# Two score groups in a row in four PSUM banks, and the second head's P v summed at the pair's end

## The chip, the cores and the metric

The kernel runs on one core of a Trainium2 chip. A time is the device time of one execution in microseconds (us); the number for a kernel is the median of its runs. The core has five engines, each with an instruction stream of its own, in order: TensorE (PE, with its weight loads shown as PEld), ScalarE (ACT), VectorE (DVE), GpSimd (POOL) and SyncE (SP), which here only issues DMAs. Matrix products go to PSUM, eight banks of 128 partitions by 512 fp32 values; ACT and DVE read them there.

## The reference

```
q, k, v: (8 batches, 12 heads, 448 tokens, 64), fp32;  g_q, g_k: (64)
q_n = q / rms(q) * g_q ;  k_n = k / rms(k) * g_k
scores = q_n k_n^T / 8 ;  attn = softmax(scores) ;  o = attn v
x = o, as 3584 tokens by 768
h = x w_in  (768 by 2048) ;  g = h * cos(h) ;  y = g w_out  (2048 by 768)
```

w_in and w_out come as 64-bit floats and are turned into fp32 on the chip.

## The kernel before

Two heads of a batch make a pair; there are 48 pairs u, six a batch. The first 9 pairs (u < 9) multiply in plain fp32. The other 39 split each operand into a high and a low fp32r part and sum the products that matter.

**Scores.** The 448 queries of two heads are seven tiles of up to 128 queries by 448 keys. `score(u, j)` (line 425) makes one group: for j = 0, 1, 2 tile j of the first head (array rows 0 to 63) and tile j + 4 of the second (rows 64 to 127), side by side in the array; for j = 3 tile 3, which holds the rest of both heads and takes all 128 rows. A group of a later pair has three passes (qhi khi, ql khi, qhi kl), so six matmuls for two tiles. A tile fills one PSUM bank "S"; DVE takes its row minimum (`rowmin`, L447; the scores are negated), ACT exponentiates it to SBUF (`expo`, L456), and the bank is free again. There are three S banks; for the first six pairs every fourth tile goes to the bank "ph" instead (`place`, line 416).

**P v.** The seven tiles of P are transposed on PE in four blocks of keys kc, into the two-bank tile PT (`transp`, L483: four transposes of the first head, three of the second; one more in one block for the row sums, L485). Of each half ACT copies the high part (`pt_high`, L494) and DVE takes the low part (`pt_low`, L502, L504). Then `av(u, kc, hh)` (L514) adds block kc to the output O of head hh, one or two matmuls a call; a head's bank of O is summed over seven matmuls. In pairs u < 9 there is no low part, and `av_whole` (L522) does both heads in one bank. `x_half` (ACT, L540) and `x_sum` (DVE, L545) take O out of PSUM, and the result goes to one of the six slots xf of its batch.

**PSUM.** S has three banks, PT two, O two (one a head), ph one: eight.

**First layer.** `ffn1` multiplies a batch's x by w_in, 16 blocks of 18 matmuls in the bank ph (L573 to L575), among the attention of the next batch. So PE has other work in nearly every wait of an attention step. Batch 7's first layer and the whole second layer (seven block products in place of eight, L648 to L650) follow after the attention.

**Weights.** `weights2` prepares w_out meanwhile: eight rounds, in each four quarters are decoded and mixed into seven 128 by 384 operands, each split into high (ACT, L269) and low (POOL, L272) in the buffer "wv" and stored to DRAM.

**Order.** `Plan` (line 28) is a list scheduler that runs when the program is built: each step has an engine, a cost, a due time, and keys that it reads and writes; a free engine takes, of its ready steps, the one with the earliest due time. The result is the fixed order of all five instruction streams. `RING` gives the number of buffers of each name; a step waits for the users of the buffer's last instance. `prepare(u)` brings k and q of a pair: POOL multiplies k by its norm (`k_norm`, L370), for the later pairs ACT rounds it to khi (`k_high`, L373) and POOL makes kl (`k_low`, L377). khi and kl have two buffers each, so those of a pair can be made while the pair before still multiplies.

Of the kernel before, what the change touches and what calls it, by code (L numbers as in the profile page):

```python
# [126 lines left out]
def tile_attention_moe(  # L127
# [11 lines left out]
    nc = tc.nc  # L139
# [24 lines left out]
    ps_s = att.enter_context(tc.tile_pool(name="ps_s", bufs=3, space=PSUM))  # L164
# [24 lines left out]
    def g_fold():  # L189
# [54 lines left out]
    X1, X2, Y1, Y2, SS = range(5)  # L244
# [14 lines left out]
    def v_mix(k, to, a, c, op):  # L259
        if to == SS and (k, SS) not in mix:  # L260
            mix[(k, SS)] = apool.tile([128, HM], F32, tag="wx", name=f"wx{k}_{SS}", bufs=RING["wx"])
        nc.gpsimd.tensor_tensor(mix[(k, to)], mix[(k, a)], mix[(k, c)], op)
# [152 lines left out]

    def place(u, n):
        i = 7 * min(u, NP) + (n if u < NP else 0)
        if u < NP:
            return ("ph", i // 4) if i % 4 == 3 else ("S", 3 * (i // 4) + i % 4)
        return ("S", i - i // 4 + 7 * (u - NP) + n)  # L420

    NSP = 7 * NP // 4


    def score(u, j):
        d = pair[u]
        ops = (("qhi", "khi"), ("ql", "khi"), ("qhi", "kl"))[: 1 if u in S32 else 3]
        if j == 0:
            tl(u, "sm", [128, 4, NQT], F32)
        tiles = (3,) if j == 3 else (j, j + 4)  # L430
        for n, t in enumerate(tiles):
            tag = place(u, 2 * j + n)[0]
            pool = ps_h if tag == "ph" else ps_s
            d["S", t] = pool.tile([128, 512], F32, tag=tag, name=f"S{u}_{t}")
        for n, (a, c) in enumerate(ops):
            for t in tiles:
                p0, p1 = (0, 128) if t == 3 else (0, 64) if t < 3 else (64, 128)
                nc.tensor.matmul(  # L438
                    d["S", t][:, :S], d[a][p0:p1, j * 128 : j * 128 + 128], d[c][p0:p1, :],
                    start=(n == 0), stop=(n == len(ops) - 1),  # L440
                )
# [45 lines left out]
    def pt_high(u, kc, hh):  # L487
        d = pair[u]
        dt = F32 if u in A32 else F32R
        hi = d["hi", kc, hh] = apool.tile([128, S], dt, tag="hi", name=f"hi{u}_{kc}_{hh}", bufs=RING["hi"])  # L490
# [5 lines left out]
    def pt_low(u, kc, hh):  # L496
# [3 lines left out]
        if kc < 3:  # L500
            lo = d["lo", kc, hh] = apool.tile([128, S], F32R, tag="lo", name=f"lo{u}_{kc}_{hh}", bufs=RING["lo"])
# [13 lines left out]

    def av_whole(u, kc):
        d = pair[u]
        if kc == 0:
            d["O"] = ps_o.tile([128, 2, 512], F32, tag="O", name=f"O{u}")
        rows, c = ((128, 0), (128, 1), (128, 3), (64, 2))[kc]  # L520
        for hh in range(2):
            nc.tensor.matmul(  # L522
                d["O"][64 * hh : 64 * hh + 64, 0, :S], d["vs"][:rows, 0, hh * NVC + c],
# [6 lines left out]
    def x_out(u):  # L530
        xf[u] = xpool.tile([128, S], F32, tag=f"xf{u % NP}", name=f"xf{u}")
        nc.vector.tensor_tensor(xf[u], pair[u]["O"][:, 0, :S], pair[u]["rs"], ALU.mult)
        del pair[u]

    def x_half(u, hh):
        O = pair[u]["O"]
# [3 lines left out]
        nc.scalar.copy(xf[u][a : a + 64], O[c : c + 64, hh, :S])  # L540

    def x_sum(u, hh):
        a = 64 * hh
        x = xf[u][a : a + 64]
        nc.vector.tensor_tensor(x, pair[u]["O"][a : a + 64, hh, :S], x, ALU.add)  # L545
# [141 lines left out]
    SPLIT = 50.0  # L687
    WAHEAD = 100.0
# [24 lines left out]
    def weights2(k):  # L713
        span = (base(NU - 2) - base(3 * NP)) / NH
        d0 = base(3 * NP) + k * span
        x = [("wx", 5 * k + m) for m in range(5)]
        for m in (X1, X2, Y1, Y2):
# [3 lines left out]
            if f64:  # L721
# [4 lines left out]
        todo = ((1, X1, None), (2, Y1, None), (4, Y2, None), (5, SS, (X2, Y2, ALU.add)), (7, X2, (X1, X2, ALU.subtract)),  # L726
                (6, SS, (SS, X1, ALU.subtract)), (3, Y1, (Y1, SS, ALU.subtract)))
# [335 lines left out]
```

## Time and profile before

| | us |
|---|---|
| median of 3 runs | 1446.78 (1446.69 to 1447.9) |
| the profiled execution | 1444.56 |
| its span, first to last instruction | 1442.7 |
| PE busy, of the span | 1398.2 (97%) |
| DVE, ACT, POOL busy | 1022.5, 1000.2, 931.0 (71%, 69%, 65%) |

The profile shows one execution. "Busy" counts an engine's instructions from start to end. PE's matmuls overlap: one lasts 0.37 us and the next starts 0.2 us after it, so a later start than that shows as a gap only when it is large. For PE the distance from start to start is what is to be read. A wait of PEld is one of the weight load that stands ahead of a matmul. The attention with its first layers fills the span from about 10 to about 955 us, the rest is the last batch's first layer and the second layer.

### The profile page before, as it was taken

The numbers are of one execution on the slowest core, as the hardware profiler recorded it, in microseconds if no ns is written. First come the engines' busy times: TensorE is split into PE (matmuls) and PEld (weight loads), VectorE is DVE, ScalarE is ACT, GpSimd is POOL, SyncE is SP. The second block draws the span as 40 slices with busy tenths as digits, with TensorE's granted clock in tenths as the row PEclk, the third lists the DMA queues.
The fourth block names the chain that finished last, engine by engine and source line by source line (L and its number), as shares of the span: only waits on it lengthen the run. The fifth ranks groups of instructions, "written<-read, shape, count | busy, mean of one in ns | idle before, by whom it ended". The sixth has DMA issues, their size and how long they took to land.

```text
span 1442.7 us, 22453 instructions
## 1 busy us (share of the span) xinstructions
PE 1398.2 (97%) x7361; PEld 1154.5 (80%) x7361; DVE 1022.5 (71%) x1649; ACT 1000.2 (69%) x2058; POOL 931.0 (65%) x722
## 2 busy tenths in 40 slices
PE   6999999999999999999999999999999999999998
PEld 2445688887888888788788888889899899899897
DVE  7778986677778686878767555437876967867921
ACT  5776677667777877777776676547776786776741
POOL 5667867666887968787675663101386585676673
PEclk9999999999999999999999999999999999999999
DMA  6787444565667566666556432149579489389372
GB/s 207 216 265 230 154 125 144 157 169 182 208 201 230 190 197 217 190 208 202 180 169 188 163 123 85 47 138 354 190 238 344 137 262 338 125 295 325 114 229 100
DMA packets 154453, 282.63 MB, mean 196 GB/s; under 512 B 31760, under 2 KB 102368, under 8 KB 154336
## 3 DMA queue, kind: packets, MB, share of 16 engines
q1 hardware_dynamic: 154336, 281.20, 61.2%
q8 instruction: 58, 0.95, 0.3%
q14 instruction: 59, 0.48, 0.1%
HBM read 218.24 MB, written 62.89 MB: 195 GB/s over the span
## 4 chain that ended last, share of the span: by engine, by line
PE 67%; DVE 13%; ACT 6%; DMA 5%; issue 4%; POOL 4%; SPq 0%; ACTq 0%; DVEq 0%; POOLq 0%
PE ph L573 8%; PE PT L483 8%; PE ph L574 8%; PE ph L575 8%; PE O L514 7%; PE S L438 7%; PE y L649 7%; PE y L650 6%; PE y L648 6%; DMA hb<-h_d 3%; DVE lo L502 2%; ACT hi L494 2%; POOL glo L633 1%; PE O L522 1%; DVE sm L447 1%
## 5 line engine op out<-in xcount | busy, mean ns | idle before, releaser
L573 PE MATMUL ph<-xs,wi 128*128 128x448 f32 x768 | 298.6, 389 | 1.7 <-ACT he L585 1.6
L574 PE MATMUL ph<-xs,wi 128*128 128x448 f32 x768 | 281.2, 366 | 0.0
L575 PE MATMUL ph<-xs,wi 128*128 128x448 f32 x768 | 281.1, 366 | 0.0
L456 ACT ACTIVATE P<-S,sm 128x448 f32<-128x448 f32 x336 | 213.3, 639 | 87.5 <-DVE sm L447 73.5
L649 PE MATMUL y<-glo,wo 128*128 128x448 f32 x672 | 247.3, 368 | 6.0 <-POOL glo L633 6.0
L650 PE MATMUL y<-ghi,wo 128*128 128x448 f32 x672 | 246.8, 367 | 0.0
L648 PE MATMUL y<-ghi,wo 128*128 128x448 f32 x672 | 246.8, 367 | 0.0
L494 ACT CAST hi<-PT 128x448 fp32r<-128x448 f32 x312 | 153.2, 536 | 70.8 <-PE PT L483 35.7
L447 DVE TENSOR_REDUCE sm<-S 128x1 f32<-128x448 f32 x322 | 187.5, 612 | 15.8 <-PE S L438 15.0
L483 PEld LDWEIGHTS PT<-ident,P 128*128 128x128 f32 x1344 | 155.5, 141 | 49.1 <-issue 25.2
L502 DVE TENSOR_TENSOR lo<-PT,hi 128x448 fp32r<-128x448 f32 x234 | 135.1, 617 | 82.9 <-ACT hi L494 79.0
L483 PE MATMUL PT<-ident,P 128*128 128x128 f32 x1344 | 185.8, 276 | 2.7 <-DVE hi L492 1.3
L573 PEld LDWEIGHTS ph<-xs,wi 128*128 128x128 f32 x768 | 144.6, 188 | 32.5 <-issue 13.2
L575 PEld LDWEIGHTS ph<-xs,wi 128*128 128x128 f32 x768 | 144.4, 188 | 12.5
L574 PEld LDWEIGHTS ph<-xs,wi 128*128 128x128 f32 x768 | 145.0, 189 | 9.9 <-issue 0.6
L649 PEld LDWEIGHTS y<-glo,wo 128*128 128x128 f32 x672 | 126.6, 188 | 18.5 <-POOL glo L633 7.5
L648 PEld LDWEIGHTS y<-ghi,wo 128*128 128x128 f32 x672 | 126.6, 188 | 11.4
L650 PEld LDWEIGHTS y<-ghi,wo 128*128 128x128 f32 x672 | 126.6, 188 | 11.2
L306 POOL TENSOR_TENSOR r<-r,nhalf 128x14 f32<-128x14 f32 (+1 forms) x50 | 127.6, 2553 | 12.3 <-DVE r L324 8.5
L438 PE MATMUL S<-khi,qhi 64*128 64x448 f32 x399 | 117.9, 521 | 7.6 <-ACT P L456 4.4
L514 PE MATMUL O<-hi,vs 128*128 128x448 f32 x312 | 105.0, 386 | 2.9 <-DVE hi L504 0.9
L377 POOL TENSOR_TENSOR kl<-kd,khi 128x448 fp32r<-128x448 f32 x39 | 49.0, 1255 | 80.7 <-ACT khi L373 66.4
(225 smaller groups left out, 2755.2 us busy)
## 6 DMA issues: line engine op xcount, KB each, us to landing
wo<-wo_d SPq DMA_DIRECT2D x88, 768.0 KB
h_d<-he SPq DMA_DIRECT2D x128, 224.0 KB
hb<-h_d SPq DMA_DIRECT2D x64, 448.0 KB
wo_d<-wv SPq DMA_DIRECT2D x56, 384.0 KB
sd<-sd SPq DMA_DIRECT2D x46, 448.0 KB
vd<-v SPq DMA_DIRECT2D x78, 160.0 KB
qd<-qT SPq DMA_DIRECT2D x48, 256.0 KB
raw<-w_in SPq DMA_DIRECT2D x16, 768.0 KB
```

What stands on the lines that cost most here:

```text
L438: nc.tensor.matmul(d["S", t][:, :S], d[a][p0:p1, j * 128 : j * 128 + 128], d[c][p0:p1, :], start=(n == 0), stop=(n == len(ops) - 1),)
L447: nc.vector.tensor_reduce(least, d["S", t][:, :S], axis=AX.X, op=ALU.min)
L456: nc.scalar.activation(tl(u, f"P{t}", [128, S], F32, "P"), d.pop(("S", t))[:, :S], AF.Exp, bias=sm[:, 1, t : t + 1], scale=-1.0, accum_out ...
L483: nc.tensor.transpose(pt[:, t * 128 : t * 128 + 128], src, ident)
L494: nc.scalar.copy(hi, pt[:, hh * S : hh * S + S])
L514: nc.tensor.matmul(O, st, d.pop((what, kb, hh)), start=(kc + n == 0), stop=(kc + n == 4))
L573: nc.tensor.matmul(ph[:, :S], whi, x2[:, 0, :], start=(cc == 0), stop=False)
L574: nc.tensor.matmul(ph[:, :S], whi, x2[:, 1, :], start=False, stop=False)
L575: nc.tensor.matmul(ph[:, :S], wlo, x2[:, 0, :], start=False, stop=(cc == NCC - 1))
L648: nc.tensor.matmul(y, whi, hi, start=(k == 0 and chain < 2), stop=False, skip_group_check=chain == 2)
L649: nc.tensor.matmul(y, whi, lo, start=False, stop=False, skip_group_check=chain == 2)
L650: nc.tensor.matmul(y, wlo, hi, start=False, stop=(k == NH - 1), skip_group_check=chain == 2)
```

## The change

For the 39 later pairs, groups 0 and 1 are made by one step, twelve matmuls in a row into four S banks (`groups`, `score`); the pairs u < 9 keep their four groups. S has four banks. O keeps one bank, for the first head. The second head's seven P v matmuls are one step at the end of the pair (`av_second`), into an S bank that it takes in turn with the scores (`SPOTS`). The buffers of the high and low parts are now separate for the two heads, and larger for the second (hi 2 and 4, lo 1 and 3, in place of 4 and 2 in common). To make room in SBUF, khi and kl go from two buffers to one, wx from five to four (the fifth, SS, is replaced by sums in place in Y2), and wv from two to one. Costs and due times of the attention steps change: groups 3 us apart instead of 4, key blocks 3.5 instead of 4.

```diff
-    ps_s = att.enter_context(tc.tile_pool(name="ps_s", bufs=3, space=PSUM))
+    ps_s = att.enter_context(tc.tile_pool(name="ps_s", bufs=4, space=PSUM))
...
-        "sd": 1, "r": 5, "rkb": 1, "rqb": 1, "kd": 1, "kl": 2, "khi": 2, "qd": 1, "ql": 2, "qhi": 2, "vd": 1, "vs": 2, "S": 3, "sm": 3, "P": 12,
-        "hi": 4, "lo": 2, "O": 1, "xf": 6, "rs": 1, "rt": 1, "ph": 1, "he": 2, "wf": 2,
-        "wx": 5, "wv": 2,
+        "sd": 1, "r": 5, "rkb": 1, "rqb": 1, "kd": 1, "kl": 1, "khi": 1, "qd": 1, "ql": 2, "qhi": 2, "vd": 1, "vs": 2, "S": 4, "sm": 3, "P": 12,
+        "hi0": 2, "hi1": 4, "lo0": 1, "lo1": 3, "O": 1, "xf": 6, "rs": 1, "rt": 1, "ph": 1, "he": 2, "wf": 2,
+        "wx": 4, "wv": 1,
...
+    for u in range(NU):
+        for n in range(8 if u >= len(A32) else 7):
+            what = (u, n)
+            if n == 7:
+                what = (u - 1, 7) if u > len(A32) else None
+            if what is None:
+                continue
+            i = 7 * u + n
+            tag = "ph" if u < NP and i % 5 == 4 else "S"
+            SPOTS[what] = (tag, NSPOT[tag])
+            NSPOT[tag] += 1
...
+    def groups(u):
+        return ((0,), (1,), (2,), (3,)) if u < 9 else ((0, 1), (2,), (3,))
+
+    def score(u, js):
...
+        for j in js:
+            tiles = (3,) if j == 3 else (j, j + 4)
...
-        if kc == 0 and hh == 0:
-            d["O"] = ps_o.tile([128, 2, 512], F32, tag="O", name=f"O{u}")
-        O = d["O"][:, hh, :S]
+        if kc == 0:
+            pool, tag = (ps_s, "S") if hh else (ps_o, "O")
+            d["O", hh] = pool.tile([128, 512], F32, tag=tag, name=f"O{u}_{hh}")
+        O = d["O", hh][:, :S]
...
+    def av_second(u):
+        for kc in range(4):
+            av(u, kc, 1)
+
...
+    LATEB = 16.0
...
-        todo = ((1, X1, None), (2, Y1, None), (4, Y2, None), (5, SS, (X2, Y2, ALU.add)), (7, X2, (X1, X2, ALU.subtract)),
-                (6, SS, (SS, X1, ALU.subtract)), (3, Y1, (Y1, SS, ALU.subtract)))
+        todo = ((1, X1, None), (2, Y1, None), (4, Y2, None), (5, Y2, (X2, Y2, ALU.add)), (7, X2, (X1, X2, ALU.subtract)),
+                (6, Y2, (Y2, X1, ALU.subtract)), (3, Y1, (Y1, Y2, ALU.subtract)))
...
-        step = 4.0
+        step = 3.0
...
-            dk = D1 + 4 * kc
+            dk = D1 + 3.5 * kc
...
-            for hh in range(2):
-                n, m = 8 * u + 2 * kc + hh, 6 * u + 2 * kc + hh
-                r = [[("hi", n), ("lo", m)], [("hi", n), ("lo", m)], [("lo", m)], [("hi", n), ("hi", n - 2)]][kc]
-                add(PE, 0.21 if kc == 2 else 0.41, dk + 4, av, u, kc, hh, lead=0.6, r=[("vs", u, hh)] + r, w=[("O", u, hh)])
+            r = [[("hi0", n), ("lo0", m)], [("hi0", n), ("lo0", m)], [("lo0", m)], [("hi0", n), ("hi0", n - 1)]][kc]
+            add(PE, 0.21 if kc == 2 else 0.41, dk + 4, av, u, kc, 0, lead=0.6, r=[("vs", u, 0)] + r, w=[("O", u)])
+        if u not in A32:
+            r = [("hi1", 4 * u + kc) for kc in range(4)] + [("lo1", 3 * u + kc) for kc in range(3)]
+            add(PE, 1.44, D1 + LATEB, av_second, u, lead=0.6, r=[("vs", u, 1)] + r, w=[place(u, 7)])
```

How the order of the instructions moves is shown at three places. In the rows a name such as S24_0 is pair 24's score tile 0, O26 pair 26's output, hi26_1_0 the high part of its key block 1 for its first head; the last number is the buffer's.

PE, the groups of pair 24, in the kernel before: group 1 between the transposes of pair 23 and the first layer (group 0 stands 24 matmuls earlier).

```order
L485 MATMUL PT_98<-ident_88,sm23_4991 7x128
L438 MATMUL S24_1_5357<-khi24_4925,qhi24_4937 128x448
L438 MATMUL S24_5_5358<-khi24_4925,qhi24_4937 128x448
L438 MATMUL S24_1_5357<-khi24_4925,ql24_4944 128x448
L438 MATMUL S24_5_5358<-khi24_4925,ql24_4944 128x448
L438 MATMUL S24_1_5357<-kl24_4939,qhi24_4937 128x448
L438 MATMUL S24_5_5358<-kl24_4939,qhi24_4937 128x448
L573 MATMUL ph2_12_5308<-xs_484,wi12_1802 128x448
```

The same pair's groups 0 and 1 on PE in the changed kernel (L450 is the score matmul there):

```order
L450 MATMUL S24_0_5223<-khi24_5171,qhi24_4956 128x448
L450 MATMUL S24_4_5224<-khi24_5171,qhi24_4956 128x448
L450 MATMUL S24_0_5223<-khi24_5171,ql24_4968 128x448
L450 MATMUL S24_4_5224<-khi24_5171,ql24_4968 128x448
L450 MATMUL S24_0_5223<-kl24_5187,qhi24_4956 128x448
L450 MATMUL S24_4_5224<-kl24_5187,qhi24_4956 128x448
L450 MATMUL S24_1_5231<-khi24_5171,qhi24_4956 128x448
L450 MATMUL S24_5_5232<-khi24_5171,qhi24_4956 128x448
L450 MATMUL S24_1_5231<-khi24_5171,ql24_4968 128x448
L450 MATMUL S24_5_5232<-khi24_5171,ql24_4968 128x448
L450 MATMUL S24_1_5231<-kl24_5187,qhi24_4956 128x448
L450 MATMUL S24_5_5232<-kl24_5187,qhi24_4956 128x448
```

Nothing stands between the two groups any more. Over the program PE has 117 separate runs of 64-row score matmuls of the later pairs before, and 78 now; of the pairs u < 9 it has 26 and 21; and 214 and 196 runs of transposes.

PE, P v of pair 26's key block 1 in the kernel before, with the transposes of block 2 behind it:

```order
L514 MATMUL O26_6091<-hi26_1_0_6128,vs26_5790 128x448
L514 MATMUL O26_6091<-lo26_1_0_6158,vs26_5790 128x448
L514 MATMUL O26_6091<-hi26_1_1_6141,vs26_5790 128x448
L514 MATMUL O26_6091<-lo26_1_1_6164,vs26_5790 128x448
L483 MATMUL PT_98<-ident_88,P026_5832 128x128
```

PE, the end of pair 25 in the changed kernel (L527 is P v there):

```order
L527 MATMUL O25_0_5788<-hi25_3_0_5916,vs25_5452 128x448
L527 MATMUL O25_0_5788<-hi25_2_0_5857,vs25_5452 128x448
L527 MATMUL O25_1_5963<-hi25_0_1_5755,vs25_5452 128x448
L527 MATMUL O25_1_5963<-lo25_0_1_5779,vs25_5452 128x448
L527 MATMUL O25_1_5963<-hi25_1_1_5810,vs25_5452 128x448
L527 MATMUL O25_1_5963<-lo25_1_1_5823,vs25_5452 128x448
L527 MATMUL O25_1_5963<-lo25_2_1_5886,vs25_5452 128x448
L527 MATMUL O25_1_5963<-hi25_3_1_5927,vs25_5452 128x448
L527 MATMUL O25_1_5963<-hi25_2_1_5867,vs25_5452 128x448
L590 MATMUL ph3_2_5920<-xs_447,wi2_761 128x448
```

The second head's matmuls, before beside the first head's in every key block, now stand together after the last block.

ACT, where khi of pair 27 is made, in the kernel before:

```order
L557 CAST xs_484<-xf23_5515 128x448
L373 CAST khi27_5716<-kd27_5494 128x448
L390 ACTIVATE qhi27_5723<-qd27_5571,gs_93 128x512
L269 CAST wv2_7_5731<-wx2_1_5131 128x384
L494 CAST hi24_3_0_5739<-PT_98 128x448
L494 CAST hi24_3_1_5747<-PT_98 128x448
L456 ACTIVATE P625_5754,sm25_5501<-S25_6_5649,sm25_5501 128x448
```

And in the changed kernel (L371 makes khi, L468 is the exponential):

```order
L468 ACTIVATE P226_5930,sm26_5761<-S26_2_5895,sm26_5761 128x448
L468 ACTIVATE P626_5940,sm26_5761<-S26_6_5896,sm26_5761 128x448
L371 CAST khi27_5951<-kd27_5695 128x448
L468 ACTIVATE P326_5955,sm26_5761<-S26_3_5936,sm26_5761 128x448
L557 COPY xf25_5971<-O25_0_5788 64x448
```

khi of pair 27 was made while the exponentials of pair 25 were still to come; now it stands among the last exponentials of pair 26, behind the last score matmul that reads pair 26's khi.

## Rows read from the trace of the kernel before

**Rows 1.** The page, busy us, share of the span and instructions of each engine

```profile
PE 1398.2 (97%) x7361; PEld 1154.5 (80%) x7361; DVE 1022.5 (71%) x1649; ACT 1000.2 (69%) x2058; POOL 931.0 (65%) x722
```

**Rows 2.** Stretches: length, busy us of PE, PEld, DVE, ACT, POOL, PE's clock, DMA

```profile
0.00:160.00 160.00, 136.75 (x620) 69.66 (x621) 127.75 (x205) 109.58 (x243) 110.52 (x86) 0.98 0.75 226
160.00:840.00 680.00, 670.91 (x3783) 553.08 (x3781) 509.34 (x853) 497.03 (x1166) 498.09 (x470) 1.00 0.59 182
840.00:930.00 90.00, 89.86 (x517) 74.59 (x516) 49.22 (x90) 56.90 (x137) 32.78 (x36) 1.00 0.25 81
```

**Rows 3.** PE in order of time, one score group: start, us, instruction

```profile
522.99 0.37 PE L575 MATMUL ph<-xs,wi 128*128 128x448 f32 x1
523.28 0.47 PE L438 MATMUL S<-khi,qhi 64*128 64x448 f32 x2
523.59 0.36 PE L438 MATMUL S<-khi,ql 64*128 64x448 f32 x2
523.80 0.37 PE L438 MATMUL S<-kl,qhi 64*128 64x448 f32 x2
524.10 0.47 PE L514 MATMUL O<-hi,vs 128*128 128x448 f32 x1
524.40 0.37 PE L514 MATMUL O<-lo,vs 128*128 128x448 f32 x1
524.60 0.36 PE L514 MATMUL O<-hi,vs 128*128 128x448 f32 x1
```

**Rows 4.** PE in order of time, from transposes to first layer and to scores

```profile
513.97 0.93 PE L483 MATMUL PT<-ident,P 128*128 128x128 f32 x7
514.65 0.45 PE L573 MATMUL ph<-xs,wi 128*128 128x448 f32 x1
514.94 0.36 PE L574 MATMUL ph<-xs,wi 128*128 128x448 f32 x1
...
885.66 0.93 PE L483 MATMUL PT<-ident,P 128*128 128x128 f32 x7
886.52 0.47 PE L438 MATMUL S<-khi,qhi 64*128 64x448 f32 x2
886.83 0.36 PE L438 MATMUL S<-khi,ql 64*128 64x448 f32 x2
```

**Rows 5.** Weight loads of the score group's second pass, whole span: busy us, mean ns

```profile
L438 PEld LDWEIGHTS S<-khi,ql 64*128 64x128 f32 x234 | 23.0, 186 | 0.0
```

**Rows 6.** Waits of PEld, 160 to 930 us: us, times, longest us

```profile
PEld O L514 <- DVE lo L502: 13.7, 40, 0.9
PEld PT L483 <- DVE lo L502: 5.2, 17, 0.4
PEld S L438 <- ACT P L456: 4.2, 7, 1.6
PEld O L514 <- ACT xf L540: 3.5, 8, 0.5
```

**Rows 7.** Groups of instructions, whole span: busy us, mean ns, idle before and releaser

```profile
L456 ACT ACTIVATE P<-S,sm 128x448 f32<-128x448 f32 x336 | 213.3, 639 | 87.5 <-DVE sm L447 73.5 <-PE PT L483 7.0 <-DVE S L449 5.7
L447 DVE TENSOR_REDUCE sm<-S 128x1 f32<-128x448 f32 x322 | 187.5, 612 | 15.8 <-PE S L438 15.0
L373 ACT CAST khi<-kd 128x448 fp32r<-128x448 f32 x39 | 22.2, 570 | 4.1 <-PE S L438 3.9
L377 POOL TENSOR_TENSOR kl<-kd,khi 128x448 fp32r<-128x448 f32 x39 | 49.0, 1255 | 80.7 <-ACT khi L373 66.4 <-DMA rawo<-w_out 5.4 <-DMA wo_d<-wv 3.3
L370 POOL TENSOR_TENSOR khi<-kd,rkb 128x448 f32<-128x448 f32 x7 | 10.6, 1508 | 0.0
L306 POOL TENSOR_TENSOR r<-r,nhalf 128x14 f32<-128x14 f32 x46 | 121.7, 2646 | 3.8
L540 ACT COPY xf<-O 64x448 f32<-64x448 f32 x78 | 41.2, 528 | 26.5 <-PE O L514 16.3 <-DVE xf L545 8.6 <-POOL xs L559 0.8
L545 DVE TENSOR_TENSOR xf<-O,xf 64x448 f32<-64x448 f32 x78 | 48.5, 622 | 37.9 <-ACT xf L540 30.9 <-ACT P L456 3.8 <-PE ph L575 1.7
```

More of the change, by code (lines that the diff above doesn't have):

```diff
@@ L413, in v_low @@
         nc.gpsimd.tensor_tensor(vs[:, :, 1, :], pair[u].pop(f"vd{hh}"), vs.bitcast(F32)[:, :, 0, :], ALU.subtract)
-    def place(u, n):
[L417 to L425, printed above, removed]
+    SPOTS = {}
+    NSPOT = {"S": 0, "ph": 0}
+    for u in range(NU):
[9 more added lines that the diff above has]
+            NSPOT[tag] += 1
@@ L426, in score @@
+    SPOTS[NU - 1, 7] = ("S", NSPOT["S"])
+    NSP = NSPOT["ph"]
+    def place(u, n):
+        return SPOTS[u, n]
+    def groups(u):
+        return ((0,), (1,), (2,), (3,)) if u < 9 else ((0, 1), (2,), (3,))
+    def score(u, js):
         d = pair[u]
         ops = (("qhi", "khi"), ("ql", "khi"), ("qhi", "kl"))[: 1 if u in S32 else 3]
-        if j == 0:
+        if js[0] == 0:
             tl(u, "sm", [128, 4, NQT], F32)
[L430 to L441, printed above, removed]
+        for j in js:
+            tiles = (3,) if j == 3 else (j, j + 4)
+            for n, t in enumerate(tiles):
+                tag = place(u, 2 * j + n)[0]
+                pool = ps_h if tag == "ph" else ps_s
+                d["S", t] = pool.tile([128, 512], F32, tag=tag, name=f"S{u}_{t}")
+            for n, (a, c) in enumerate(ops):
+                for t in tiles:
+                    p0, p1 = (0, 128) if t == 3 else (0, 64) if t < 3 else (64, 128)
+                    nc.tensor.matmul(
+                        d["S", t][:, :S], d[a][p0:p1, j * 128 : j * 128 + 128], d[c][p0:p1, :],
+                        start=(n == 0), stop=(n == len(ops) - 1),
+                    )
@@ L715, in weights2 @@
         d0 = base(3 * NP) + k * span
-        x = [("wx", 5 * k + m) for m in range(5)]
+        x = [("wx", 4 * k + m) for m in range(4)]
         for m in (X1, X2, Y1, Y2):
@@ L788, in attend @@
         b, cc = divmod(u, NP)
[L789 removed]
+        step = 3.0
         lead = 0.0 if u < NP else None
[L791 to L795 removed]
+        for js in groups(u):
+            dj = D0 + step * js[0]
+            todo = [(n, t) for j in js for n, t in enumerate((3,) if j == 3 else (j, j + 4), 2 * j)]
+            keys = [place(u, n) for n, _ in todo]
+            cost = (0.97 if js[0] < 3 else 0.86) if u in S32 else (1.0 if js[0] < 3 else 0.68)
+            cost += (0.88 if u in S32 else 0.62) * (len(js) - 1)
             operands = ("qhi", "khi") if u in S32 else ("qhi", "ql", "khi", "kl")
[L797 to L798 removed]
+            r = [(n, u) for n in operands if u >= NFIRST or n != "khi"]
+            r += [("khi", u, 0), ("khi", u, 1)] if u < NFIRST else []
+            add(PE, cost, dj, score, u, js, lead=lead, r=r, w=keys)
+            for (n, t), key in zip(todo, keys):
                 if u < NFIRST:
```

53 lines of the change are left out of this document (21 added, 32 removed).

## Prediction, written before the changed kernel ran

> **What bounds the kernel now.** I read the page first. PE is busy 97% of the span, the next engine 71% [rows 1]. Then the stretches: from 160 to 930 us, where the 39 split pairs run, PE is busy 760.8 of 770 us, at the full granted clock of 2.4 GHz, while DVE, ACT and POOL have 558.6, 553.9 and 530.9 us of work, 69 to 73% [rows 2]. So PE sets the end there, and a change can gain only by taking time out of PE's own stream. That time has three forms: matmuls (the same number before and after: the program computes the same), switches between kinds of matmul, and waits. "Busy" hides the last two, since a matmul's record covers a late start of the next, so I read PE in order of time, from start to start. The waits come from the list of who waited for whom, on PE's weight loads.
>
> **What a score group costs.** In one kind of work matmuls start 0.205 us apart. Around a group of 64-row scores the steps are 0.29 into it, 0.31 from its first pass to the second, 0.21 to the third, 0.30 out of it, 0.30 from the first matmul behind it to the next, then 0.20 [rows 3]. Over five plain steps that is 0.085 + 0.105 + 0.005 + 0.095 + 0.095 = 0.38 us lost per group, half at each side. Behind transposes it is the same: seven transposes and the step to a second matmul take 0.68 + 0.29 = 0.97 us where first-layer matmuls follow, 0.86 + 0.31 = 1.17 where scores follow [rows 4], 0.20 more, against 0.19 at the entry in [rows 3]. So what stands beside the group does not matter, and it is the count of groups that costs.
>
> **Groups 0 and 1 in a row.** The order has 78 runs of such scores in the later pairs where it had 117: 39 fewer, one a pair. 39 x 0.38 = 14.8 us, all of it on PE, which bounds this stretch. What the rows do not show is the step from the last pass of group 0 to the first of group 1: same shape, other weights. Bounds: 0.205 as between passes 2 and 3, or 0.31 as between passes 1 and 2. I take the first, because the step from the second pass to the third also changes both halves' weights and costs 0.21; with the other the term is 39 x (0.38 - 0.105) = 10.7.
> A rule speaks against this. A score pass loads its two halves in 0.186 us each [rows 5], and the step from pass 2 to pass 3, which needs both anew, is still 0.21: the loads are hidden behind the matmuls. The Trainium skill ("TensorE: Matmul & The Clock Gate", Part 3: Packing small matmuls, on what overlaps) says that a weight load overlaps a matmul in flight only where it is for other rows of the array, and a pass holds all rows. The trace does not bear that out inside a group; if it held at the seam alone, the term would be 39 x (0.38 - 0.19) = 7.4, and the time 1431.
>
> **Fewer returns from transposes, fewer fp32 groups.** PE has 196 runs of transposes for 214. Each return to other work costs 0.29 - 0.205 = 0.085 [rows 4]: between 0 and 18 x 0.085 = 1.5; I take 1.0. The pairs u < 9 have 21 runs of score pairs for 26; at most 5 x 0.38 = 1.9 if an fp32 switch costs what a split one does, at least 0; I take 1.0.
>
> **The waits from 160 to 930 us.** PE is idle for 770 - 760.8 = 9.2 us there [rows 2]; the weight loads waited 13.7 us for low parts in front of P v, 5.2 for low parts in front of transposes, 4.2 for an S bank, 3.5 for the copy that frees O [rows 6], 26.6 in all. The second sum counts the ordinary pause of a load as well, the first misses what a running matmul covers; I take the middle, 18 us, two thirds of what the list says. What of it goes:
> - The second head's P v no longer waits block by block. All its operands but the last block's are old when it starts, and the seven matmuls stand behind two of the first head (the second place of the order). That is about half of the waits for low parts in front of P v: 6.9 x 2/3 = 4.6.
> - An S bank came free and was wanted again after as little as 2.3 us of PE work, by counting rows between two users; with four banks the least is 4.5. Minimum and exponential take 0.61 + 0.64 us [rows 7] plus hand-overs. The 4.2 go almost whole: 2.5 after the same cut.
> - The waits before transposes stay: PT still has one buffer.
> What is new: the second head's O holds an S bank until ACT has copied and DVE added (0.53 + 0.62 [rows 7]), and the next pair's group of four tiles wants that bank 2.9 to 5.4 us of PE work later. Behind one exponential and one minimum the chain is 0.53 + 0.62 + 0.64 + 0.61 = 2.4 and hand-overs; a quarter of the pairs are near 2.9, so 10 waits of 0.1 us or so: 1.
> Net 4.6 + 2.5 - 1 = 6. Bounds: all 18 gone, or 6 more than now.
>
> **One buffer of khi and kl.** khi of pair u may be written only when the last score of pair u - 1 has read the old one; then ACT 0.57, POOL 1.26 [rows 7], then the first scores of pair u. ACT's queue shows it (third place): the cast that stood two pairs ahead now stands among the last exponentials of the pair before. Behind it on ACT wait the exponential of tile 3 and the copies of O; if the cast waits for PE, they do. Of PE work the order leaves between the last score of a pair and the first of the next at least 3.9 us (6.4 in the middle; 5.1 before pair 27), all work that needs neither khi nor kl, and this hides 1.83 us and two hand-overs. I count 0; if the cover were gone the price is in the rivals. In the pairs 2 to 8 the step is POOL's product alone, 1.5 us [rows 7]; the tightest place is before pair 8, eight transposes and two fp32 matmuls, about as long as that. At up to 0.7 us in each of these seven pairs 5 us would be lost; PE is idle 23.3 us of the first 160 as it is [rows 2], of which the extra S bank may take some. I take 0, between 5 lost and 3 gained.
>
> **wx, wv and the sums in Y2.** One buffer of wv makes each operand wait for the store of the one before, so the 56 stores spread: the last, behind block 12 of batch 5's first layer before, now stands behind block 5 of batch 6's, nine of 112 blocks later (some 65 us, an estimate from 112 blocks in about 860 us). From 840 to 930 us POOL was busy 32.8 of 90 [rows 2], so the work fits there, and the second layer reads the stores only afterwards: 0. The second layer itself is not touched.
>
> **Sum.** 14.8 + 1.0 + 1.0 + 6 = 22.8 us. The profiled execution took 1444.56, so 1421.8; the median of the runs shown is 2.2 above it: 1424.0.
>
> **Rivals.**
> - The merge gives less. The seam costs 0.105, and the burst of four tiles brings as many waits as the two heads' split removes. For it: four exponentials (0.64 each) come due at once on ACT, between which the high parts stand; against: the order leaves at least 4.5 us between users of a bank. 10.7 + 1, with no gain of waits: 1446.8 - 12 = 1435. The Trainium skill ("TensorEngine Tiling (Array Packing)", PSUM Bottleneck) warns that row tiling speeds the products and not what empties PSUM; 73% on DVE is what the trace has on it.
> - The waits go nearly all. 15 of the 18, and 3 in the first pairs: 14.8 + 1 + 1 + 15 + 3 = 34.8, 1412. For it: no operand of the second head is fresh. Against: the first head's chain over PT keeps its length.
> - khi and kl late: slower. The chain from the last score of a pair over ACT and POOL to the next pair's first score is 1.83 us, but behind one exponential (0.64) and one power (2.65 [rows 7]) it is 5.1, as long as the cover before pair 27. PE would stand at the first score of a pair, and every queue behind it. It outweighs the merge from 16.8 / 45 = 0.37 us a pair on; at 0.6 us over 45 pairs, 27 - 16.8 = 10 lost: 1457. Against: the order gives 6.4 us in the middle, and POOL is 69% busy.
> - Another engine takes what PE gives back, so nothing shows: 1446. For it POOL's 73% from 160 to 840 us; against it that no engine but PE is above 75% there.
> That the change does not do what it says is excluded by the order: the 39 merged runs are in it.
>
> **How the numbers follow.** 1424 has 0.58 (its own range 1416 to 1431), 1435 has 0.20, 1412 has 0.12, 1457 has 0.06, 1446 has 0.04. The range of 8 in 10 takes the likeliest, most of the next and half of the third: 1411 to 1438. A change of less than 0.2% (2.9 us) can't be told from none by a measurement of this kernel. Faster by more than that: the first three, 0.90; within it 0.04; slower 0.06.
>
> **What will show it.** The seam: in PE's order of time the step from the last pass of group 0 to the first of group 1 at 0.2 us, and twelve matmuls in six steps with 0.38 us of excess in all. PE's busy time down by some 15 to 20 us in the attention's stretch, which should end near 930 instead of 955. Waits of weight loads for low parts about a third shorter in front of P v, for an S bank nearly gone. I am wrong if the first score of a pair waits for kl or for POOL (rival three), if the seam takes 0.3 or more, or if the first 160 us grow by more than 5.

## The result, and the profile after

| | before | after |
|---|---|---|
| median, us | 1446.74 (4 runs, 1445.98 to 1447.90) | 1422.62 (4 runs, 1419.13 to 1424.15) |
| ratio of the times | | 0.9831, 95% interval 0.9816 to 0.9846 |
| the profiled execution, its span | 1444.56, 1442.7 | 1419.13, 1417.3 |

The changed kernel is 24.1 us faster by the medians; 1424.0 had been forecast. The profiled executions differ by 25.4 us in their spans, and where these went is read below. The time came out as the forecast's sum did, but not by its terms: one term was right, one had the wrong sign, and one of the same size was missing. The last two belong together, as is shown below the table.

The page's line of busy times, changed kernel, to be read beside [rows 1]:

```profile
PE 1365.7 (96%) x7361; PEld 1158.6 (82%) x7361; DVE 1023.9 (72%) x1649; ACT 997.3 (70%) x2058; POOL 927.8 (65%) x722
```

PE's busy time fell by 32.5 us with the same 7361 matmuls, the span by 25.4. The other engines did what they did before. The stretches of [rows 2] in the changed kernel (columns as there):

```profile
0.00:160.00 160.00, 137.74 (x693) 75.45 (x693) 126.75 (x210) 113.86 (x260) 101.28 (x87) 1.00 0.74 231
160.00:840.00 680.00, 664.05 (x3837) 569.81 (x3837) 522.85 (x874) 505.40 (x1181) 510.23 (x473) 0.99 0.59 181
840.00:930.00 90.00, 88.80 (x507) 76.98 (x507) 44.97 (x82) 51.47 (x124) 30.58 (x33) 1.00 0.30 100
```

In the first 160 us PE started 693 matmuls where it had started 620, at the same busy time: that is the first surprise. From 160 to 840 us it was idle for 15.95 us where it had been idle for 9.1: that is the second. 

One merged pair of groups, PE in order of time in the changed kernel (start, us, instruction), to be read beside [rows 3]:

```profile
300.49 0.47 PE L450 MATMUL S<-khi,qhi 64*128 64x448 f32 x2
300.80 0.36 PE L450 MATMUL S<-khi,ql 64*128 64x448 f32 x2
300.99 0.38 PE L450 MATMUL S<-kl,qhi 64*128 64x448 f32 x2
301.20 0.37 PE L450 MATMUL S<-khi,qhi 64*128 64x448 f32 x2
301.40 0.38 PE L450 MATMUL S<-khi,ql 64*128 64x448 f32 x2
301.60 0.38 PE L450 MATMUL S<-kl,qhi 64*128 64x448 f32 x2
301.91 0.47 PE L590 MATMUL ph<-xs,wi 128*128 128x448 f32 x1
302.21 0.36 PE L591 MATMUL ph<-xs,wi 128*128 128x448 f32 x1
302.41 0.36 PE L592 MATMUL ph<-xs,wi 128*128 128x448 f32 x1
```

The seam is the step from 300.99 to 301.20: 0.21 us, a plain step. The slow steps are those of one group (0.31 from first to second pass, 0.31 out, 0.30 behind it), now paid once for two groups. Over the 39 merged runs the seam was 0.20 or 0.21 in 38 and 0.31 in one.

Waits of weight loads from 160 to 930 us, changed kernel (us, times, longest), to be read beside [rows 6]:

```profile
PEld PT L495 <- DVE lo L514: 20.4, 41, 2.9
...
PEld O L527 <- DVE lo L514: 7.7, 14, 1.3
...
PEld O L527 <- DVE hi L516: 4.9, 5, 2.4
...
PEld S L450 <- POOL kl L375: 1.0, 1, 1.0
PEld S L450 <- ACT P L468: 0.9, 3, 0.3
```

In front of P v (L527) the waits for low parts went from 13.7 to 7.7, for an S bank from 4.2 to 0.9, and those for the copy that frees O are gone from the list. But in front of the transposes (L495) they went from 5.2 to 20.4: PT is free again only when DVE has taken the low parts out of it. The single wait for kl is all that one buffer of khi and kl shows at the scores.

**Where the 25.4 us went.** From PE's starts in the trace I counted, for both kernels, a plain 0.2045 us for each pass of scores, P v and first layer, 0.109 for each transpose, and 0.38 for each run of 64-row scores of the later pairs [rows 3]; what is left over is waits and everything else. The fp32 work of the first nine pairs is taken as one piece: the time up to its last matmul, less the later kinds of work that PE did meanwhile.

| us | before | after | change |
|---|---|---|---|
| up to the last fp32 matmul (at 170.3 and 150.1), less 24.6 and 19.0 of other work and 0.38 for each of its 3 and 2 runs | 144.6 | 130.3 | -14.3 |
| plain steps of the later pairs and the first layer | 802.6 | 802.5 | 0 |
| 117 and 78 runs of 64-row scores, 0.38 each | 44.5 | 29.6 | -14.8 |
| waits and the rest | 26.1 | 32.6 | +6.5 |
| second layer, first to last matmul | 420.5 | 417.9 | -2.6 |

The sum is -25.2. The first and the fourth row must be read together. Counted in the same way, some 1 us of the waits and the rest (W below) before and 12 after lie between the last fp32 matmul and the end of batch 0's first layer (at 246 and 242 us). Some 11 of the 14.3 us gained up to the last fp32 matmul are lost again there, so that the two stretches together gain some 3. Behind them W is about 25 and 21. PE from 160 to 240 and from 240 to 930 us, in the kernel before and then in the changed one (columns as in [rows 2]):

```profile
160.00:240.00 80.00, 79.46 (x455) 64.19 (x453) 64.40 (x102) 60.04 (x136) 60.73 (x54) 1.00 0.45 135
240.00:930.00 690.00, 681.30 (x3845) 563.49 (x3844) 494.16 (x841) 493.89 (x1167) 470.14 (x451) 1.00 0.56 174
```

```profile
160.00:240.00 80.00, 75.06 (x409) 63.12 (x410) 70.55 (x104) 57.73 (x128) 59.24 (x52) 0.96 0.42 123
240.00:930.00 690.00, 677.79 (x3935) 583.67 (x3934) 497.27 (x851) 499.14 (x1178) 481.57 (x455) 1.00 0.57 177
```

PE's idle time is 0.5 and 4.9 us in the first of these stretches, 8.7 and 12.2 in the second. W, which goes by starts, also holds the late starts that a running matmul covers; so in the second stretch it could fall while idle time rose.

The attention with its first layers, up to the first matmul of the second layer, ended at 1017.7 us before and at 995.2 after. Of the second layer's 2.6 nothing may be read: its instructions are the same in all fourteen kernels below, and in their profiled executions it took between 417.2 and 425.3 us. Differences of a few us in one execution are therefore no finding here, and where it can be done I read the end of the attention beside the median.

### The profile page after: what moved, and what is told of

It reads as the page before. It is cut to its first block, busy times and chain, and to the rows that moved or that the text cites. A ratio compares the mean times of both kernels' runs of the same rounds, so it can differ in the third digit from the quotient of the medians.

```text
span 1417.3 us, 22398 instructions
## 1 busy us (share of the span) xinstructions
PE 1365.7 (96%) x7361; PEld 1158.6 (82%) x7361; DVE 1023.9 (72%) x1649; ACT 997.3 (70%) x2058; POOL 927.8 (65%) x722
## 5 line engine op out<-in xcount | busy, mean ns | idle before, releaser
L468 ACT ACTIVATE P<-S,sm 128x448 f32<-128x448 f32 x336 | 213.0, 643 | 65.4 <-DVE sm L459 59.2
L506 ACT CAST hi<-PT 128x448 fp32r<-128x448 f32 x312 | 152.6, 535 | 90.0 <-PE PT L495 44.5
L495 PEld LDWEIGHTS PT<-ident,P 128*128 128x128 f32 x1344 | 152.2, 140 | 57.0 <-DVE lo L514 20.4
L495 PE MATMUL PT<-ident,P 128*128 128x128 f32 x1344 | 182.8, 276 | 12.3 <-DVE lo L514 7.4
L459 DVE TENSOR_REDUCE sm<-S 128x1 f32<-128x448 f32 x322 | 184.0, 611 | 13.4 <-PE S L450 13.3
L450 PE MATMUL S<-khi,qhi 64*128 64x448 f32 x399 | 106.7, 486 | 4.3 <-ACT khi L341 2.3
L527 PE MATMUL O<-hi,vs 128*128 128x448 f32 x312 | 103.8, 385 | 3.2 <-DVE hi L516 3.1
L602 ACT COPY he<-ph 128x448 f32<-128x448 f32 x128 | 68.3, 534 | 46.8 <-PE ph L592 35.1
```

The source lines that it names most:

```text
L459: nc.vector.tensor_reduce(least, d["S", t][:, :S], axis=AX.X, op=ALU.min)
L468: nc.scalar.activation(tl(u, f"P{t}", [128, S], F32, "P"), d.pop(("S", t))[:, :S], AF.Exp, bias=sm[:, 1, t : t + 1], scale=-1.0, accum_out ...
L495: nc.tensor.transpose(pt[:, t * 128 : t * 128 + 128], src, ident)
L506: nc.scalar.copy(hi, pt[:, hh * S : hh * S + S])
L527: nc.tensor.matmul(O, st, d.pop((what, kb, hh)), start=(kc + n == 0), stop=(kc + n == 4))
```

## Experiments

All kernels in one table: the median with its ratio to the kernel before, run on the same chip (the medians come from several chips, so two rows are best compared by their ratios), and from the profiled execution the terms of the table above (P1 the first pairs' piece, R runs x 0.38, W waits and rest) and the start of the second layer, which is the end of the attention.

| kernel | median, us | ratio [95%] | P1 | R | W | attention ends |
|---|---|---|---|---|---|---|
| before | 1446.74 | 1 | 144.6 | 44.5 | 26.1 | 1017.7 |
| changed | 1422.62 | 0.9831 [0.9816, 0.9846] | 130.3 | 29.6 | 32.6 | 995.2 |
| four_groups | 1429.29 | 0.9881 [0.9845, 0.9916] | 132.8 | 41.4 | 24.9 | 1001.6 |
| late_head_only | 1446.57 | 0.9998 [0.9977, 1.0020] | 138.7 | 44.5 | 33.2 | 1018.8 |
| small_buffers | 1460.19 | 1.0106 [1.0081, 1.0130] | 145.0 | 44.5 | 40.3 | 1032.3 |
| khi_one | 1459.60 | 1.0092 [1.0064, 1.0121] | 146.3 | 44.5 | 41.8 | 1035.1 |
| wv_one | 1453.66 | 1.0044 [1.0025, 1.0063] | 146.2 | 44.5 | 33.9 | 1027.2 |
| due_times_only | 1441.04 | 0.9954 [0.9930, 0.9977] | 141.3 | 44.5 | 18.9 | 1007.2 |
| old_due_times | 1435.12 | 0.9912 [0.9886, 0.9937] | 148.9 | 29.6 | 28.9 | 1010.0 |
| first_pairs_due | 1422.20 | 0.9820 [0.9803, 0.9837] | 130.0 | 29.6 | 30.6 | 992.8 |
| due_times_earlier | 1422.55 | 0.9817 [0.9789, 0.9844] | 136.6 | 29.6 | 27.1 | 995.9 |
| buffers_back | 1428.70 | 0.9866 [0.9840, 0.9892] | 134.2 | 29.6 | 34.4 | 1000.8 |
| decode_costs | 1428.68 | 0.9859 [0.9826, 0.9892] | 133.9 | 29.6 | 36.8 | 1002.8 |
| merge_1_2 | 1430.51 | 0.9866 [0.9840, 0.9891] | 130.7 | 29.6 | 38.4 | 1001.3 |

### The merge alone: four_groups

```diff
-        return ((0,), (1,), (2,), (3,)) if u < 9 else ((0, 1), (2,), (3,))
+        return ((0,), (1,), (2,), (3,))
```

> The changed kernel with four score groups planned apart for all pairs; four S banks, the late second head and all else as changed. Its order has 109 runs of 64-row scores (eight pairs still have two groups side by side by chance) where the changed kernel has 78. Theory (each run costs PE 0.38 us): 31 x 0.38 = 11.8 us slower than the changed kernel, about 1434. Rival (the gain came from the banks, the late sum and the due times, not from the switches): within 4 us of 1423.

1429.29 us, 6.7 above the changed kernel; the two intervals just touch. The order happens to put two groups side by side in eight places, so there are 109 runs for 78, and 31 x 0.38 = 11.8 us were to come back. The attention ended 6.4 us later: 11.8 of runs and 2.5 of the first pairs more, 7.7 of waits less. These waits in the four-group kernel, 160 to 930 us, weight loads:

```profile
PEld PT L495 <- DVE lo L514: 12.9, 39, 0.7
PEld O L527 <- DVE lo L514: 11.6, 23, 1.4
```

In front of the transposes they are 12.9 for 20.4, with a longest of 0.7 for 2.9. So the switches cost what the step counts say, and by this one pair of executions over half of that comes back as waits, 6 of the 7.7 us before the end of batch 0's first layer. These 31 runs are worth about 7 us by the medians, not 11.8. How much of that is the merge's own is not shown: the orders differ elsewhere too, and decode_costs below moves W by 4.2 us without touching a group.

### The late second head alone: late_head_only

The second head's O has its own bank again, S three, the groups are four; the small buffers, the due times and the late P v stay.

```diff
-    ps_s = att.enter_context(tc.tile_pool(name="ps_s", bufs=4, space=PSUM))
+    ps_s = att.enter_context(tc.tile_pool(name="ps_s", bufs=3, space=PSUM))
...
-            pool, tag = (ps_s, "S") if hh else (ps_o, "O")
+            pool, tag = (ps_o, "O1") if hh else (ps_o, "O")
```

> The changed kernel with four groups, three S banks as before, and a bank of its own for the second head's O, which is still summed at the pair's end; buffers and due times as changed. 117 runs of 64-row scores. Theory (switches carry most of the gain, late sum and fourth bank change the waits little): 39 x 0.38 = 14.8 slower than the changed kernel, 1437, so some 9 faster than before, which is the first pairs' and the due times' share. Rival (the late sum removes the waits for low parts as the prediction said): 6 us better than that, 1431.

1446.57: no gain at all, where both expectations had one. Something in this bundle costs what the rest gives; the small buffers, which cost 13 us in the kernel before (next section), are the first suspect, but no run has the late head without them. The step from here to four_groups is the fourth S bank shared with the second head's O: 0.9998 to 0.9881, 17 us at the medians, of which 5.9 are in P1, 8.3 in W and 3.1 in eight runs fewer.

### What the smaller buffers cost in the kernel before: small_buffers, khi_one, wv_one

```diff
-        "sd": 1, "r": 5, "rkb": 1, "rqb": 1, "kd": 1, "kl": 2, "khi": 2, "qd": 1, "ql": 2, "qhi": 2, "vd": 1, "vs": 2, "S": 3, "sm": 3, "P": 12,
+        "sd": 1, "r": 5, "rkb": 1, "rqb": 1, "kd": 1, "kl": 1, "khi": 1, "qd": 1, "ql": 2, "qhi": 2, "vd": 1, "vs": 2, "S": 3, "sm": 3, "P": 12,
...
-        "wx": 5, "wv": 2,
+        "wx": 4, "wv": 1,
```

(with the sums in Y2 as in the change); khi_one has the first pair of lines alone, wv_one the second.

> The kernel before with the smaller buffers alone: khi and kl one buffer, wv one, wx four with the sums in place. Theory (the order leaves enough PE work between a pair's last score and the next pair's first): within 3 us of before, 1447. Rival (khi and kl come late): at least 5 us slower, with waits of score weight loads for kl in the list.

> The kernel before with one buffer of khi and of kl instead of two, nothing else. The small buffers together cost 13 us (1460 against 1447). Theory A (khi and kl late: the third rival of the prediction): 1457 or more here, and the waits of P v for low parts, 13.7 us before, grow as with all small buffers, because ACT's cast holds up the high parts. Theory B (the weights' buffer wv): within 4 us of 1447.

> The kernel before with one buffer of wv and four of wx (sums in place), khi and kl two as before. Theory A (khi and kl late): within 4 us of 1447. Theory B (each of the 56 casts into wv waits in ACT's queue for the store before it): 1457 or more. If both come out near 1453, the price is shared or is that of another order.

All three are slower, by 13.3, 13.4 and 7.5 us against the kernel before on the same chip. The prediction had counted 0 for both. khi_one is as dear as both together, so the two don't add. The prediction's third rival had put 27 us on the single khi and kl (1457 with the merge's gain taken off); half of that price is seen here, but not by the rival's mechanism. The waits for the cast to khi, whole span, in the kernel with one khi:

```profile
L373 ACT CAST khi<-kd 128x448 fp32r<-128x448 f32 x39 | 22.5, 577 | 4.8 <-PE S L438 4.7
```

4.8 us of idle time on ACT against 4.1 in [rows 7], and between 160 and 930 us neither PE nor its weight loads wait for khi or kl. The waits stand elsewhere, PE's weight loads from 160 to 930 us:

```profile
PEld O L514 <- DVE lo L502: 20.9, 39, 2.2
...
PEld O L514 <- DVE hi L504: 6.9, 16, 3.0
```

That is 20.9 for 13.7 and 6.9 for 1.6 in front of P v. So the single buffer does not stop PE at the scores; it gives the list scheduler another order, in which P v waits longer for the low parts. The instructions themselves are no slower: from 160 to 930 us a high part takes 0.536 us and a low part 0.617 in both kernels. Why the scheduler's order is worse was not settled.

### Does that cost remain in the changed kernel: buffers_back

```diff
-        "sd": 1, "r": 5, "rkb": 1, "rqb": 1, "kd": 1, "kl": 1, "khi": 1, "qd": 1, "ql": 2, "qhi": 2, "vd": 1, "vs": 2, "S": 4, "sm": 3, "P": 12,
+        "sd": 1, "r": 5, "rkb": 1, "rqb": 1, "kd": 1, "kl": 2, "khi": 2, "qd": 1, "ql": 2, "qhi": 2, "vd": 1, "vs": 2, "S": 4, "sm": 3, "P": 10,
```

> The changed kernel with two buffers of khi and kl again, paid for in SBUF with 10 buffers of P in place of 12. Theory (the single buffers still cost something in the changed kernel, because they narrow the planner's choice, as the 13 us in the kernel before): 1410 to 1417, with the waits on PE and its weight loads for low parts between 160 and 930 us below those of the changed kernel. Rival (the late second head and the earlier due times already give the room that the single buffers took): within 4 of the changed kernel's 1422.6, and the same sum of waits.

1428.70, ratio 0.9866: not faster, rather some us slower (the intervals overlap). The theory's 1410 to 1417 did not come. That the single buffers of khi and kl cost nothing in the changed kernel is not shown by this: P has ten buffers in place of twelve, which may cost as much as the two buffers give. The rival's "within 4" is not shown either.

### Due times: due_times_only, old_due_times, first_pairs_due, due_times_earlier

due_times_only is the kernel before with the new due times, old_due_times the changed kernel with the old ones:

```diff
-        step = 4.0
+        step = 3.0
...
-            dk = D1 + 4 * kc
+            dk = D1 + 3.5 * kc
```

> The kernel before with the new due times alone: score groups 3 us apart in the plan, key blocks 3.5. Theory A (the gain of 8 us in the first pairs comes from the due times): 1447 - 8 = 1439. Theory B (it comes from the fourth S bank): within 3 us of 1447. PE's runs of transposes fall from 214 to 194 here, worth at most 1.7 us by 0.085 each.

> The changed kernel with the due times of before: score groups 4 us apart in the plan, key blocks 4. The new due times alone made the kernel before 5.9 us faster. Theory (they bring the gain in the first pairs also here): 1428 to 1431, with the first 160 us holding less of the program. Rival (the fourth bank does it): within 3 us of 1423.

In the kernel before, two changed numbers give 0.9954, some 6 us. Taken out of the changed kernel they cost 12 us, 0.9912 with an interval clear of the changed kernel's. In both the first pairs move (P1 144.6 to 141.3, and from the old due times to the new in the changed kernel 148.9 to 130.3; some of the 148.9 is the clock's, which was granted at 0.94 in the first 160 us of that execution, 1.00 in the changed kernel's). When PE starts the first split score shows it, in the kernel before, the changed one, and the changed one with the old due times:

```profile
150.74 0.36 PE L438 MATMUL S<-khi,ql 64*128 64x448 f32 x2
```

```profile
133.92 0.37 PE L450 MATMUL S<-khi,ql 64*128 64x448 f32 x2
```

```profile
152.98 0.37 PE L450 MATMUL S<-khi,ql 64*128 64x448 f32 x2
```

With the old due times that score is back where it was. In the kernel before, though, the larger part of what the new due times brought lies behind the first pairs: W fell from 26.1 to 18.9, P1 only by 3.3, in an execution that was 6.3 us below its kernel's median. To see whether the later pairs matter, first_pairs_due has the new due times in the pairs u < 9 alone:

```diff
-        step = 3.0
+        step = 3.0 if u in A32 else 4.0
...
-            dk = D1 + 3.5 * kc
+            dk = D1 + (3.5 if u in A32 else 4) * kc
```

> The changed kernel with its earlier due times (score groups 3.0 us apart, key blocks 3.5) in the pairs u < 9 alone; the 39 later pairs have the old ones (4.0 and 4). Theory (what the due times bring comes from the first pairs, where PE starts more work before 160 us): the first split score near 134 us as in the changed kernel, the attention's last first-layer matmul at 995 to 999, the time 1419 to 1426, and the waits of weight loads of transposes for low parts between 160 and 930 us near 2, as with the old due times, against 20.4. Rival (the later pairs bring it, by their order): as with the old due times everywhere, the last first-layer matmul at 1006 to 1010 and the time 1432 to 1438.

It is the changed kernel's time, 1422.20, with the attention's end at 992.8, earlier than was expected. In the changed kernel, what the due times bring comes from the first nine pairs. Its stretch up to 160 us, and its waits of weight loads from 160 to 930 us:

```profile
0.00:160.00 160.00, 140.56 (x700) 77.28 (x700) 128.80 (x211) 113.95 (x260) 102.86 (x88) 0.98 0.74 232
```

```profile
PEld ph L590 <- ACT he L602: 17.6, 20, 2.5
...
PEld O L527 <- DVE hi L516: 6.5, 6, 2.4
PEld O L527 <- DVE lo L514: 6.2, 9, 1.7
...
PEld PT L495 <- DVE lo L514: 2.7, 9, 0.3
```

The transposes' waits are gone (2.7 for 20.4), as was expected: key blocks 3.5 us apart had caused them. Yet W is only 2.0 lower, since the first layer now waits for the copy of the bank ph (L602), 17.6 for 3.4. In the later pairs waits change their place more than their sum.

due_times_earlier goes on in the same direction, groups 2.5 and blocks 3.0 apart:

> The changed kernel with its due times a further step earlier: score groups 2.5 us apart for 3.0, key blocks 3.0 for 3.5. Theory (earlier due times gain because they keep PE fed in the first 160 us and leave room before P v, 12.5 us for the step before): 3 to 8 more, 1415 to 1420. Rival (the step before took all there was): within 3 of 1422.6, or slower by new waits in front of P v.

0.9817 with an interval around the changed kernel's 0.9831: no difference. The first step had taken all there was; P1 is worse by 6.3, W better by 5.5.

### Which groups are merged: merge_1_2

```diff
-        return ((0,), (1,), (2,), (3,)) if u < 9 else ((0, 1), (2,), (3,))
+        return ((0,), (1,), (2,), (3,)) if u < 9 else ((0,), (1, 2), (3,))
```

> The changed kernel with groups 1 and 2 in a row in place of groups 0 and 1; the runs of 64-row score matmuls are 78 as before. Theory (it is the count of switches alone that counts): 1422.6 within 4, with the same 41 us of switches from start to start. Rival (the pair that is merged sets how much PE work lies between a transpose and the P v that needs its low part; in this order the tenth of the first head's low parts with the least room has 2.3 us of it, against 2.9 in the changed kernel, and between two pairs' scores there are 1.9 us at the least against 3.9): 5 to 12 slower, 1428 to 1435, in waits for low parts.

1430.51, attention's end 6.1 later with the same 78 runs and the same first pairs: W is 5.8 higher. The intervals of the two ratios overlap by 0.0006, so the 5 to 8 us are likely rather than shown. Weight loads, 160 to 930 us:

```profile
PEld PT L495 <- DVE lo L514: 16.3, 32, 2.0
PEld O L527 <- DVE lo L514: 14.4, 23, 1.6
```

In front of P v they wait 14.4 where the changed kernel waits 7.7. That speaks for the rival, that it is not the count alone; but another order by itself can shift as much, as the next experiment shows.

### The two large waits: decode_costs

The largest waits of the changed kernel's attention, but for one at its very start, are at 162 and 197 us. PE there, then DVE in the stretch before the second (start, us, instruction, idle before and releaser):

```profile
159.37 0.37 PE L450 MATMUL S<-kl,qhi 64*128 64x448 f32 x2
162.26 0.98 PE L495 MATMUL PT<-ident,P 128*128 128x128 f32 x7 [2.52 <-DVE lo L514]
...
194.66 0.36 PE L527 MATMUL O<-hi,vs 128*128 128x448 f32 x1
197.07 0.61 PE L527 MATMUL O<-hi,vs 128*128 128x448 f32 x1 [2.05 <-DVE hi L516]
197.48 0.57 PE L590 MATMUL ph<-xs,wi 128*128 128x448 f32 x1
197.85 0.57 PE L591 MATMUL ph<-xs,wi 128*128 128x448 f32 x1
198.22 0.57 PE L592 MATMUL ph<-xs,wi 128*128 128x448 f32 x1
```

```profile
191.40 1.65 DVE L220 SCALAR_TENSOR_TENSOR wf<-raw,wf 128x768 int32<-128x768 int32 x1
192.97 1.65 DVE L216 TENSOR_SCALAR wf<-raw 128x768 int32<-128x768 int32 x1
194.66 1.83 DVE L218 SCALAR_TENSOR_TENSOR wf<-raw,wf 128x768 int32<-128x768 int32 x1
196.41 1.14 DVE L516 TENSOR_TENSOR hi<-PT,hi 64x448 fp32r<-64x448 f32 x2
```

Three steps of the decoding of w_in stand on DVE in front of the low part (L516) that P v needs, and take 1.65 to 1.83 us where the scheduler counts 0.6, 1.05 and 1.0. The experiment gives it the means between 60 and 240 us, 0.86, 1.31 and 1.23; the fourth step, with a mean of 1.08, was left at 1.1:

```diff
-            for step, eng, cost in ((0, DVE, 0.6), (1, DVE, 1.05), (2, DVE, 1.0), (3, ACT, 0.92), (4, DVE, 1.1)):
+            for step, eng, cost in ((0, DVE, 0.86), (1, DVE, 1.31), (2, DVE, 1.23), (3, ACT, 0.92), (4, DVE, 1.1)):
```

> The changed kernel with the planner's costs of the four VectorE steps that decode w_in set to what they take in the trace of the changed kernel between 60 and 240 us (0.86, 1.31, 1.23 and 1.08 us for 0.6, 1.05, 1.0 and 1.1). Theory (the waits of 2.7 and 2.2 us at 162 and 197 us come from a plan that is too short there for VectorE): these two go, and the time is 4 to 6 below 1422.6, 1417 to 1419. Rival (what is gained there comes back as other waits, since another order follows everywhere): within 3 of 1422.6 or slower.

1428.68, not faster. PE's own waits from 160 to 240 us fell from 5.0 to 3.7 in all, the longest from 2.5 to 1.7. The two waits are gone or shorter, which fits the named cause without proving it, since another order follows everywhere: P1 rose by 3.6 and W by 4.2. The rival holds. The means are also below the 1.65 to 1.83 us that the steps took in front of the second wait. For all experiments here this one is a measure: three of the scheduler's costs changed by 0.23 to 0.26 us, and W moved by 4.2.

## Why the prediction was right, and where it was not

The time was right (1422.6 for 1424.0) and so was the direction. The largest term held by its mechanism; the rest came out by two errors that cancel to within 2 us, and that they do so this closely is luck.

- **Groups 0 and 1 in a row, 14.8.** Held, term and mechanism: 39 runs fewer, the seam a plain step. The rule of the Trainium skill ("TensorE: Matmul & The Clock Gate", Part 3: Packing small matmuls), that a weight load overlaps only a matmul on other rows, does not hold at the seam either: each half's load takes 0.18 to 0.19 us, and the step is 0.20. With it the seam would have been 0.39. What the sum left out is that the merge may pay back in waits: in four_groups W is 7.7 lower where the runs cost 11.8 more. How much of this is the merge's doing is not shown.
- **Fewer returns from transposes, 1.0.** Wrong in kind. Seven transposes take 0.68 us in front of other work [rows 4], some 0.08 less than 7 x 0.109 (their own step); the 0.085 that the return costs is what the last transpose saves. Fewer runs are worth nothing. The 1.0 for the five fp32 runs fewer lies inside P1 and can't be told apart there.
- **Waits from 160 to 930 us, -6.** The step that failed: W rose by 6.5, an error of 12.5. Of its parts, the S bank (4.2 to 0.9) and the low parts in front of P v (13.7 to 7.7, half as forecast) came; though due_times_only, without a late second head, shows 6.5 in front of P v as well, so they are not owed to the late head alone. One sentence that failed is that the waits before the transposes stay. They went from 5.2 to 20.4, since key blocks due 3.5 us apart ask for PT sooner: first_pairs_due, with 4 in the later pairs, has 2.7. I had written the due times down as part of the change and given them no price. These waits do not explain the 6.5, however: first_pairs_due, without them, has W only 2.0 lower and the same time. The rise lies right behind the first pairs, from some 1 us to 12 up to 242 us. The two waits at 162 and 197 us with the slow steps behind them are 7.5 of it, both for a low part in front of which VectorE was decoding w_in; the rest is open. Behind 242 us W fell by some 4, in one execution of each kernel too little to call a finding.
- **The first 160 us, 0.** Missed: -14.3, more than the forecast's own bound of 3 gained. old_due_times and first_pairs_due show the cause: the due times. But some 11 of the 14.3 return as waits right behind, so this term and the one above are in large part one shift; together they came to -7.8, where -6 and -1.0 had been forecast. Less of it comes with the fourth S bank (late_head_only to four_groups, 138.7 to 132.8). In PE's steps the largest part is in front of the fp32 P v: its 144 starts took 42.7 us before and 31.8 after. The trace of before had shown the room, 23.3 us of idle PE in this stretch [rows 2], and I had looked only for what khi's single buffer might lose there.
- **One buffer of khi and kl, wx and wv, 0.** In the changed kernel no cost is seen at the scores (one wait for kl, 1.0 us), as forecast; whether the order costs something is open, since buffers_back also took two buffers of P. In the kernel before the same edit costs 13 us by another order. The forecast's argument looked only at the chain from score to score and could not have seen that.
- **The second layer, 0.** Its 2.6 lie inside its own spread.

The rivals: the seam at 0.105 is excluded; PE as the bound holds, 96% busy with DVE at 72%; khi late did not occur. That a merge gives some waits back, the other half of the first rival, is what four_groups points to without showing it.

## What to carry to other kernels

Price every line of a change, the planner's due times too: here two numbers were worth half of the gain, and the stretch with the most idle time on the bounding engine was where they worked. A gain in one stretch must be followed into the next: most of the one in the first pairs was waited away right behind them. With a list scheduler, an edit's cost is that of the new order and is not additive: the same smaller buffers cost 13 us in one kernel, and giving khi and kl back in its successor gained nothing, so a bound from the critical chain of one step says little about them. A difference of a few us between two orders is then not yet the effect that the edit was meant to test. When a forecast is right, compare its terms with the trace before believing its reasons.

## What the runs showed of the chip

- The two large waits on PE cost more than themselves. Behind those at 162 and 197 us the steps of 448 columns took 0.37 us instead of 0.2. Stretches of the changed kernel (columns as in [rows 2], the clock third from the end):

```profile
193.00:197.00 4.00, 2.02 (x10) 1.52 (x9) 3.97 (x5) 2.82 (x4) 2.35 (x2) 1.00 0.29 84
197.00:201.00 4.00, 3.93 (x12) 3.51 (x13) 4.00 (x8) 2.59 (x7) 0.00 (x0) 0.57 0.21 63
201.00:205.00 4.00, 4.00 (x23) 3.34 (x21) 2.88 (x5) 1.92 (x5) 2.92 (x4) 1.00 0.42 108
```

  The granted clock was 0.57 there: mostly the lower level, 1.2 GHz, behind a wait in which PE stood idle. The 17 such steps behind the two waits cost 17 x 0.17 = 2.9 us beside the 2.52 and 2.05 us that PE waited.
- The same is seen in the second layer, which no edit touched, but not behind every wait. PE in the four-group kernel, then in the changed one:

```profile
1031.58 0.48 PE L666 MATMUL y<-glo,wo 128*128 128x448 f32 x1 [2.60 <-POOL glo L650]
...
1033.15 0.57 PE L667 MATMUL y<-ghi,wo 128*128 128x448 f32 x1
1033.53 0.57 PE L665 MATMUL y<-ghi,wo 128*128 128x448 f32 x1
```

```profile
1024.65 0.47 PE L666 MATMUL y<-glo,wo 128*128 128x448 f32 x1 [2.61 <-POOL glo L650]
...
1028.00 0.36 PE L667 MATMUL y<-ghi,wo 128*128 128x448 f32 x1
1028.20 0.36 PE L665 MATMUL y<-ghi,wo 128*128 128x448 f32 x1
```

  In the first, a wait of 2.60 us for POOL's low part is followed, after some plain steps, by nine slow ones of 0.35 to 0.37 us; the granted clock is 0.50 from 1034 to 1036 us. In the second, a wait of 2.61 us is followed by plain steps at a clock of 1.00. In the four-group execution one of two later waits of 2.6 us has slow steps behind it, and in the kernel before a wait of 1.87 us at 1149 us has eight. The length of the wait alone does not decide it; what does is not shown.
